# Block-sparse attention with a soft mixture of experts: value products with two heads in one matmul

## The chip, the core and the metric

The kernel runs on one NeuronCore of a Trainium2 chip. The metric is device time in microseconds (us) of one execution. The core has five engines with queues of their own: PE (TensorE, matmuls; its weight loads are listed apart as PEld), DVE (VectorE), ACT (ScalarE), POOL (GpSimd) and SP, which here only issues DMAs. They wait for one another on semaphores. PE multiplies a stationary operand (`lhsT`, loaded as weights) with a moving operand (`rhs`) whose columns stream through; contraction runs over the partitions of both, and results go to PSUM, eight banks of 512 float32 numbers for each of the 128 partitions. A product with fewer than 128 rows or weight columns uses a part of the array, a tile, and products in different tiles can run at the same time.

## The reference

Inputs are float32: `q`, `k`, `v` of shape (4, 8, 768, 64) (batches, heads, positions, head dimension) and, for the experts, `phi` (512 x 32), `w1` (8 x 512 x 1024), `w2` (8 x 1024 x 512).

```python
scores = scale * np.matmul(q, k.transpose(0, 1, 3, 2))
mask = (abs(blk_i - blk_j) <= 1) | (blk_i in (0, 23)) | (blk_j in (0, 23))
mask |= kb in sampled_blocks[qb]              # three random blocks for each query block
attn = softmax(where(mask, scores, -1e9)) @ v # heads side by side: x, 3072 x 512
logits = x @ phi
d = softmax(logits, axis=0)                   # over all 3072 rows
slot_input = d.T @ x                          # 32 slots of 512, four for each expert
slot_out[e] = relu(slot_input[e] @ w1[e]) @ w2[e]
out = softmax(logits, axis=1) @ slot_out
```

The softmaxes carry an epsilon of 1e-9. Positions are cut into 24 blocks of 32. Query blocks 0 and 23 see every key (dense); the other 22 see blocks 0 and 23, their neighbours and three sampled ones, at most eight blocks.

## The kernel before, in words

**Units.** The eight heads are four pairs; partitions 32p to 32p+31 belong to p = 0 to 3, and r = 0, 1 names the head of a pair, so one pass over r handles four heads. For every batch b there are 4 dense units (r and j, j being query block 0 or 23) and 22 sparse ones (g = 0 to 10, a pair of neighbouring query blocks, and r). `units` (L233 to L250) puts them in order: eight mixed ones by `ORDER0` or `ORDER`, then sparse ones alone. Outer blocks t = 0 to 5 are 128 rows of x: t = 0 holds the dense query blocks and the pair g = 0, each other t holds two pairs g, that is four query blocks.

**Steps of a unit.** `stage_k` (L189) copies the keys of a query block to one of four buffers `kst`: own and neighbouring blocks and the edges by POOL (L196, L201), sampled ones by ACT at addresses from registers (L205). `stage_v` (L210, L216) copies the values of the three sampled blocks by POOL to one of `NVR` = 8 buffers `vrs`. `do_qk` (L270) multiplies queries and keys, 64 rows (the head dimension of one head) to a matmul, for both r at once (L288; L277 for dense). `do_soft` takes the maximum on DVE (L304) and the exponential on ACT (L307). `do_tr` transposes 32 x 32 blocks on DVE (L326; L323 for dense), so that keys lie on partitions.

**Value products.** `av_half` (L353 to L382) computes, for one b, t and r, the product of the transposed weights with the values: for edge blocks and the pair's own two blocks (L362) 64 query rows at once, for the remaining neighbour and the sampled ones (L380) 32. The value table has 65 columns, the last one being 1, so that the sum of weights comes with it. `av_dense` (L344, L349) does it over all 24 blocks. Every matmul contracts the 32 keys of one block for one head: 32 rows, 65 columns. `avt` is one set of four banks, bank p for head p, used by all of them in turn. `av_out` (L335 to L342) adds epsilon, takes reciprocals and writes x for this r, on DVE.

**Experts' front.** `moe_front` (L385 on) takes each finished block of x: four transposes (e1, L394, evacuated by DVE), logits (e2, L439, copied by ACT to `lp`), two sums (e3, L446 and L447), the exponential on ACT and a running maximum (e3b), a transpose (e4, L463), and the product with x (e5, L478, added on DVE at L481). Some of its results lie in unused columns of `avt`.

**Order.** PE's and DVE's order is written out by hand in the loop at L568: in step n there are the value products of the unit before (`X[0]`), parts of the experts' front (`EOFF`, `X[1]`, `X[2]`), QK two units ahead, transposes of unit n, softmax. POOL, ACT and SP are ordered by the scheduler. `KSTEP` = 5 and `VSTEP` = 2 say how many units ahead keys and values are staged; at g = `KEARLY` = 4 keys and values of the next batch are loaded (`load_k`, `load_v`), in the last batch weights in their place.

**Memory and weights.** `pk` holds two tiles `ktile` and two `vtile`. The experts' weights are 64 tiles of 128 x 1024 numbers (512 KB). `NPRE` = 22 have a place of their own and are loaded during attention; three each go early to the tile `ktile` and the tile `vtile` that fall free in the last batch; the rest follows when attention ends, into `NLB` = 9 tiles `lwb` in the attention's memory and into tiles that fall free. Then come the two layers of the experts (L730, L738) and the combination (L830).

Of the kernel before, what the change touches and what calls it, by code (L numbers as in the profile page):

```python
# [21 lines left out]
P = 128  # L22
# [7 lines left out]
NBZ = NB + 1  # L30
EPS = 1e-9
# [3 lines left out]
NKST, NVR, NQ, NPTD = 4, 8, 3, 1  # L35
PB, PTB, XB = 4, 5, 2
# [4 lines left out]
KSTEP, VSTEP, EARLY = 5, 2, 4  # L41
# [13 lines left out]
NPRE, NLB = 22, 9  # L55
KW = 3
# [9 lines left out]
def attn_moe_kernel(ctx, tc, qT, kT, vtab, sampled, phi, w1, w2, out):  # L66
# [8 lines left out]

    wsrc = [w1[e, hf] for hf in range(2) for e in range(NE)]
# [12 lines left out]
    def load_wk(m, tag):  # L89
        t = pk.tile([P, KW, WP], F32, name="kw", tag=tag)  # L90
        for j in range(KW):
            load_w(m + j, None, t[:, j, :])
# [64 lines left out]
    vrs = [pst.tile([P, NR, 2 * D1], F32, name=f"vrs{n}") for n in range(NVR)]  # L157
# [52 lines left out]
    def stage_v(b, i):  # L210
# [3 lines left out]
        vf = vtile[b].rearrange("p k r d -> p k (r d)")  # L214
        for j in range(NR):
            POOL.tensor_copy(out=st[:, j:j + 1, :], in_=vf[:, ds(vals[j], 1), :])  # L216
        return st.rearrange("p j (r d) -> p j r d", r=2)
# [36 lines left out]
    def do_stage(u):  # L254
# [4 lines left out]
        if u.r == 0 and u.g == KEARLY:  # L259
# [3 lines left out]
            else:  # L263
                for j, tag in enumerate(("ktile", "vtile")):
                    load_wk(NPRE + j * KW, tag)
# [51 lines left out]
    def do_tr(u):  # L317
# [17 lines left out]
    def av_out(b, t, r, lo, hi):  # L335
        a = avt[lo:hi]
        rs = pw.tile([P, NP], F32, tag="rs", name="rs")
        DVE.tensor_scalar(out=rs[lo:hi], in0=a[:, :, D], scalar1=EPS, scalar2=None, op0=ALU.add)  # L338
        DVE.reciprocal(out=rs[lo:hi], in_=rs[lo:hi])
        x = new_x(b, t).rearrange("p (f h d) -> p f h d", f=2, h=NP)  # L340
        DVE.tensor_tensor(out=x[lo:hi, r], in0=a[:, :, 0:D],  # L341
                          in1=rs[lo:hi].unsqueeze(2).to_broadcast([hi - lo, NP, D]), op=ALU.mult)  # L342
# [10 lines left out]
    def av_half(b, t, us, r):  # L353

        vt = vtile[b]
        for n, c in enumerate((4, 5, 1, 2)):
            for p in range(NP):
                s_ = slice(32 * p, 32 * p + 32)
                for u in us:
                    o = 32 * quad(2 * u.g + 1)  # L360
                    k = (0, NB - 1, 2 * u.g + 1, 2 * u.g + 2)[n]
                    PE.matmul(avt[o:o + 64, p, 0:D1], lhsT=u.pt[s_, c].rearrange("p j q -> p (j q)"), rhs=vt[s_, k, r, :],  # L362
                              start=(n == 0), stop=False)
        for n in range(NR + 1):
            for p in range(NP):
                s_ = slice(32 * p, 32 * p + 32)
# [552 lines left out]
```

## Time and profile before

| | |
|---|---|
| three runs | 538.02, 539.32, 540.36 us (median 539.32) |
| the profiled execution | 535.25 us, span 533.5 us |
| mean granted clock of PE | 0.734 |
| instructions | 28450 |
| DMA | 60.99 MB, 114 GB/s on average |

The page of the profile gives the busy time of each engine, the span in slices, DMA queues, the chain of work that ended last, and groups of instructions by line of the kernel. "issue" is idle time in which an engine waited for nothing that the profile shows. A float32 matmul is two records of PE and two weight loads. Counts in a row that ends with a clock, a DMA share and GB/s are those of instructions that fall in that stretch. The ends of matmuls are modelled, since they are pipelined.

### The profile page before, as it was taken

Reading aid. Unit: us, or ns where it says so; the run is one execution under the profiler, and the core shown is the slowest. Engines: PE = TensorE matmul, PEld = TensorE weight load, DVE = VectorE, ACT = ScalarE, POOL = GpSimd, SP = SyncE. Lnnn points to the kernel's source line nnn. Section 1 sums busy time; section 2 is a strip of 40 time slices with the busy share of each in tenths; the row PEclk is TensorE's granted clock in tenths of the full one; section 3 lists DMA queues with packets and bytes.
Section 4 is the critical chain, followed back from the end, with each engine's and each line's share of the span. In section 5 each row is a group of like instructions: output and inputs, shape, how many; then the busy total and the mean of one; then the engine's idle time right before and its main releaser. Section 6 shows DMA issues by size and latency. Waiting matters only on the chain.

```text
span 533.5 us, 28450 instructions
## 1 busy us (share of the span) xinstructions
PE 416.5 (78%) x12629; PEld 266.3 (50%) x12629; DVE 250.2 (47%) x677; ACT 187.0 (35%) x629; POOL 125.9 (24%) x391
## 2 busy tenths in 40 slices
PE   5697378876878877779967777979687796789980
PEld 1455255554456545545655554546555454553640
DVE  2464055533654544456464445554544673550141
ACT  2435044333234333433244444332344532120140
POOL 3511033431211323232112313331113330211000
PEclk9957576769577667775687777685877656589996
DMA  8758830132200000404000004040000021099998
GB/s 300 278 161 309 326 104 24 28 127 68 75 22 23 15 17 21 142 15 137 14 23 23 15 23 143 14 130 4 24 14 23 25 78 46 10 354 409 407 346 255
DMA packets 26510, 60.99 MB, mean 114 GB/s; under 512 B 2705, under 2 KB 15122, under 8 KB 26386
## 3 DMA queue, kind: packets, MB, share of 16 engines
q1 hardware_dynamic: 26386, 59.16, 31.8%
q8 instruction: 99, 1.62, 1.2%
q14 instruction: 25, 0.20, 0.1%
HBM read 52.86 MB, written 6.29 MB: 111 GB/s over the span
## 4 chain that ended last, share of the span: by engine, by line
PE 61%; DVE 13%; issue 13%; DMA 5%; ACT 4%; ACTq 1%; SPq 0%; DVEq 0%
PE avt L380 15%; PE s L288 11%; PE avt L362 10%; PE avt L349 7%; PE sd L277 7%; DMA w<-in_w_dram 4%; DVE nm L304 3%; PE pf L730 3%; DVE ptt L326 2%; PE mlt L446 2%; DVE ptd L323 2%; PE avt L439 2%; ACT p L307 2%; PE mxt L394 2%; DVE x L341 1%
## 5 line engine op out<-in xcount | busy, mean ns | idle before, releaser
L216 POOL COPY vrs<-vtile 128x130 f32 x264 | 68.1, 295 | 209.2 <-PE avt L380 178.8
L205 ACT ACTIVATE kst<-ktile 128x128 f32 x264 | 63.8, 300 | 142.9 <-PE s L288 125.1
L380 PE MATMUL avt<-vrs,ptt 32*32 32x65 f32 x4224 | 75.8, 271 | 43.7 <-issue 43.6
L380 PEld LDWEIGHTS avt<-vrs,ptt 32*32 32x32 f32 x4224 | 63.5, 122 | 48.5 <-issue 46.6
L288 PE MATMUL s<-kst,qc 64*32 64x256 f32 x1408 | 81.0, 511 | 7.4 <-ACT p L307 4.0
L307 ACT ACTIVATE p<-s,nm 128x256 f32<-128x256 f32 x176 | 72.0, 466 | 25.1 <-DVE rs L338 15.8
L362 PE MATMUL avt<-vtile,ptt 32*64 32x65 f32 x2816 | 59.9, 278 | 13.2 <-issue 6.1
L201 POOL TENSOR_SCALAR kst<-ktile 128x384 f32<-128x384 f32 x88 | 44.0, 512 | 96.9 <-PE s L288 96.8
L304 DVE TENSOR_REDUCE nm<-s 128x2 f32<-128x512 f32 x88 | 58.8, 669 | 17.0 <-PE s L288 16.5
L362 PEld LDWEIGHTS avt<-vtile,ptt 32*64 32x64 f32 x2816 | 49.1, 171 | 34.4 <-issue 10.7
L326 DVE STREAM_TRANSPOSE ptt<-p 128x512 f32<-128x512 f32 x88 | 61.7, 701 | 0.1
L338 DVE TENSOR_SCALAR rs<-avt 128x4 f32<-128x4 f32 (+1 forms) x56 | 8.4, 150 | 90.5 <-ACT lp L312 59.0
L314 DVE COPY d<-md 128x32 f32<-128x32 f32 x23 | 4.4, 191 | 97.2 <-PE md L463 97.2
L288 PEld LDWEIGHTS s<-kst,qc 64*32 64x32 f32 x1408 | 30.0, 132 | 36.7 <-issue 17.9
L349 PE MATMUL avt<-vtile,ptd 32*64 32x65 f32 x1536 | 37.9, 279 | 11.8 <-DVE sacc L481 6.6
L277 PE MATMUL sd<-ktile,qd 64*32 64x384 f32 x256 | 41.7, 734 | 5.9 <-DMA ktile<-in_kT_dram 5.2
L349 PEld LDWEIGHTS avt<-vtile,ptd 32*64 32x64 f32 x1536 | 36.4, 192 | 14.9 <-DVE sacc L481 7.4
L301 ACT ACTIVATE pd<-sd,nb 128x384 f32<-128x384 f32 x32 | 16.8, 576 | 52.8 <-DVE nb L298 50.6
L295 DVE TENSOR_REDUCE nm<-sd 128x1 f32<-128x384 f32 x32 | 17.1, 548 | 16.8 <-PE sd L277 16.7
L341 DVE TENSOR_TENSOR x<-avt,rs 128x256 f32<-128x256 f32 (+1 forms) x56 | 23.7, 424 | 1.9
L394 PE MATMUL mxt<-ident,x 128*128 128x128 f32 x92 | 23.2, 401 | 0.0
L380 PE MATMUL avt<-vtile,ptt 32*32 32x65 f32 x1280 | 22.4, 269 | 0.4 <-issue 0.4
(104 smaller groups left out, 369.4 us busy)
## 6 DMA issues: line engine op xcount, KB each, us to landing
w<-in_w_dram SPq DMA_DIRECT2D x52, 512.0 KB, 10.2
ktile<-in_kT_dram SPq DMA_DIRECT2D x16, 384.0 KB, 5.7
kw<-in_w_dram SPq DMA_DIRECT2D x12, 512.0 KB, 5.1
qc<-in_qT_dram SPq DMA_DIRECT2D x44, 128.0 KB, 2.1
out_dram<-ob SPq DMA_DIRECT2D x20, 256.0 KB, 4.4
vtile<-in_vtab_dram SPq DMA_DIRECT2D x4, 845.0 KB, 5.6
vtile<-in_vtab_dram SPq DMA_DIRECT2D x4, 780.0 KB, 7.5
qd<-in_qT_dram SPq DMA_DIRECT2D x4, 128.0 KB, 2.2
```

What stands on the lines that cost most here:

```text
L201: POOL.tensor_scalar(out=st[:, :, w:w + 96], in0=kv[:, :, (i - 1) * BLK:(i + 2) * BLK], scalar1=SCALE, scalar2=1.0, op0=ALU.mult, op1=ALU. ...
L205: ACT.activation(out=st[:, :, o:o + BLK], in_=kv[:, :, ds(vals[j] * BLK, BLK)], func=AF.Copy, scale=SCALE)
L216: POOL.tensor_copy(out=st[:, j:j + 1, :], in_=vf[:, ds(vals[j], 1), :])
L277: PE.matmul(u.s[n][32 * p:32 * p + 32, :], lhsT=qd[s_, p, u.j, :], rhs=kt[s_, p, 384 * n:384 * (n + 1)], start=True, stop=True)
L288: PE.matmul(u.pair_of[r].s[32 * p:32 * p + 32, j, :], lhsT=q[s_, p, j, :], rhs=kst_[s_, p, :], start=True, stop=True)
L304: DVE.tensor_reduce(out=nm, in_=u.s, axis=AX.X, op=ALU.max, negate=True)
L307: ACT.activation(out=u.p[:, hf, :], in_=u.s[:, hf, :], func=AF.Exp, bias=nm[:, hf:hf + 1], scale=1.0)
L326: DVE.transpose(out=u.pt.rearrange("p k j q -> p j k q"), in_=u.p.rearrange("p j (k q) -> p j k q", k=8))
L349: PE.matmul(avt[64:128, p, 0:D1], lhsT=u.pt[s_, k].rearrange("p j q -> p (j q)"), rhs=vt[s_, k, u.r, :], start=(k == 0), stop=(k == NB - 1))
L362: PE.matmul(avt[o:o + 64, p, 0:D1], lhsT=u.pt[s_, c].rearrange("p j q -> p (j q)"), rhs=vt[s_, k, r, :], start=(n == 0), stop=False)
L380: PE.matmul(avt[o:o + 32, p, 0:D1], lhsT=u.pt[s_, c, j, :], rhs=v_, start=False, stop=(n == NR))
L394: PE.transpose(ps[:, c, :], x[:, c * P:(c + 1) * P], ident)
```

## The change

Values lie in two buffers `vbuf`, one for even and one for odd batches, with two halves a = 0, 1 of 25 x 2 x 65 numbers on every partition. The values of p stand in half p % 2; the other half is zero. POOL writes the zeros once in each buffer, four memsets of 3250 elements on 32 partitions, and `load_v` is four DMAs instead of two, of the same bytes. A value product takes partitions 64g to 64g+63 (g = 0, 1 now counts pairs of p), so two heads, and 130 columns, the two halves side by side: each head's keys meet its own values in one half and zeros in the other. The results of the two heads lie side by side.

The transposed weights of the two pairs g of an outer block share one tile of 8 x 4 x 32 (three such tiles in place of five half as large), so that the products with the edge blocks take 128 query rows at once. `avt` becomes two sets of two banks; an outer block has one set for both r, the next block the other, and `av_out` runs once for both r (in the very last block once for each). Buffers `vrs` hold both halves; there are six instead of eight, and `VSTEP` is 1. Heads are put in another order by the layout on the host, so that x comes out as before.

Of the weights 13 tiles instead of 22 have a place of their own; early groups are three in `ktile` and six in the first `vbuf`, late ones three and six in the second, and `lwb` has 11 tiles instead of 9. `c_turn` shares tiles of the new size.

```diff
-NKST, NVR, NQ, NPTD = 4, 8, 3, 1
-PB, PTB, XB = 4, 5, 2
+NKST, NVR, NQ, NPTD = 4, 6, 3, 1
+PB, PTB, XB = 4, 3, 2
-KSTEP, VSTEP, EARLY = 5, 2, 4
+KSTEP, VSTEP, EARLY = 5, 1, 4
-NPRE, NLB = 22, 9
-KW = 3
+NPRE, NLB = 13, 11
+KW = {"ktile": 3, "v0": 6, "v1": 6}
...
+    VH = NBZ * 2 * D1
+    vbuf = [pk.tile([P, 2 * VH], F32, name=f"v{n}", tag=f"v{n}", bufs=1) for n in range(2)]
...
-    vrs = [pst.tile([P, NR, 2 * D1], F32, name=f"vrs{n}") for n in range(NVR)]
+    vrs = [pst.tile([P, 2, NR, 2 * D1], F32, name=f"vrs{n}") for n in range(NVR)]
...
-    avt = psA.tile([P, NP, 512], F32, name="avt", tag="av", bufs=1)
+    avt = psA.tile([P, 2, 2, 512], F32, name="avt", tag="av", bufs=1)
...
     def load_v(b):
-        vtile[b] = pk.tile([P, NBZ, 2, D1], F32, name="vtile", tag="vtile")
-        for k0, k1 in ((0, 13), (13, NBZ)):
-            SP.dma_start(out=vtile[b][:, k0:k1], in_=vtab[b, :, k0:k1])
+        vb = vbuf[b % 2].rearrange("p (a f) -> p a f", a=2)
+        if b < 2:
+            for p in range(NP):
+                POOL.memset(vb[32 * p:32 * p + 32, 1 - p % 2, :], 0.0)
+        for p in range(NP):
+            SP.dma_start(out=vb[32 * p:32 * p + 32, p % 2, :], in_=vtab[b, 32 * p:32 * p + 32, :])
+        vtile[b] = vb.rearrange("p a (k r d) -> p a k r d", k=NBZ, r=2)
...
-            POOL.tensor_copy(out=st[:, j:j + 1, :], in_=vf[:, ds(vals[j], 1), :])
+            POOL.tensor_copy(out=st[:, :, j:j + 1, :], in_=vf[:, :, ds(vals[j], 1), :])
...
-            u.pt = pw.tile([P, 8, 2, BLK], F32, tag="ptt", name="ptt", bufs=PTB)
-            DVE.transpose(out=u.pt.rearrange("p k j q -> p j k q"), in_=u.p.rearrange("p j (k q) -> p j k q", k=8))
+            t, n = (u.g + 1) // 2, 2 * (u.g > 0 and u.g % 2 == 0)
+            if n == 0:
+                pts[u.b, t, u.r] = pw.tile([P, 8, 4, BLK], F32, tag="ptt", name="ptt", bufs=PTB)
+            u.pt = pts[u.b, t, u.r]
+            DVE.transpose(out=u.pt[:, :, n:n + 2, :].rearrange("p k j q -> p j k q"), in_=u.p.rearrange("p j (k q) -> p j k q", k=8))
...
+    def av_mm(av, o, m, g, r, lhsT, rhs, start, stop):
+        PE.matmul(av[o:o + m, g, r * 2 * D1:(r + 1) * 2 * D1].rearrange("p (a d) -> p a d", a=2),
+                  lhsT=lhsT, rhs=rhs, start=start, stop=stop)
 
     def av_dense(u):
         vt = vtile[u.b]
+        av = new_set((u.b, "d"), u.r)
         for k in range(NB):
-            for p in range(NP):
-                s_ = slice(32 * p, 32 * p + 32)
-                PE.matmul(avt[64:128, p, 0:D1], lhsT=u.pt[s_, k].rearrange("p j q -> p (j q)"), rhs=vt[s_, k, u.r, :],
-                          start=(k == 0), stop=(k == NB - 1))
-        return lambda: av_out(u.b, 0, u.r, 64, 128)
+            for g in range(2):
+                s_ = slice(64 * g, 64 * g + 64)
+                av_mm(av, 64, 64, g, u.r, u.pt[s_, k].rearrange("p j q -> p (j q)"), vt[s_, :, k, u.r, :],
+                      k == 0, k == NB - 1)
+        return (lambda: av_out(u.b, 0, av, 64, 128)) if u.r else None
...
+        for n, c in enumerate((4, 5)):
+            for g, s_ in gs:
+                av_mm(av, 0, m, g, r, pt[s_, c, 0:m // BLK].rearrange("p j q -> p (j q)"),
+                      vt[s_, :, (0, NB - 1)[n], r, :], n == 0, False)
+        for c in (1, 2):
+            for w, u in enumerate(us):
+                for g, s_ in gs:
+                    av_mm(av, 64 * w, 64, g, r, pt[s_, c, 2 * w:2 * w + 2].rearrange("p j q -> p (j q)"),
+                          vt[s_, :, 2 * u.g + c, r, :], False, False)
         for n in range(NR + 1):
-            for p in range(NP):
-                s_ = slice(32 * p, 32 * p + 32)
-                for u in us:
-                    for j in range(2):
+            for w, u in enumerate(us):
+                for j in range(2):
+                    for g, s_ in gs:
...
-                        PE.matmul(avt[o:o + 32, p, 0:D1], lhsT=u.pt[s_, c, j, :], rhs=v_,
-                                  start=False, stop=(n == NR))
-        return lambda: av_out(b, t, r, 0, 64 * len(us))
+                        av_mm(av, 64 * w + 32 * j, 32, g, r, pt[s_, c, 2 * w + j], v_, False, n == NR)
+        return (lambda: av_out(b, t, av, 0, m)) if r else None
```

More of the change, by code (lines that the diff above doesn't have):

```diff
@@ L89, in load_wk @@
     def load_wk(m, tag):
-        t = pk.tile([P, KW, WP], F32, name="kw", tag=tag)
-        for j in range(KW):
+        k = KW[tag]
+        if tag == "ktile":
+            t = pk.tile([P, k, WP], F32, name="kw", tag=tag)
+        else:
+            t = vbuf[int(tag[1])][:, 0:k * WP].rearrange("p (k f) -> p k f", k=k)
+        for j in range(k):
             load_w(m + j, None, t[:, j, :])
@@ L263, in do_stage @@
             else:
-                for j, tag in enumerate(("ktile", "vtile")):
-                    load_wk(NPRE + j * KW, tag)
+                m = NPRE
+                for tag in EARLYW:
+                    load_wk(m, tag)
+                    m += KW[tag]
         if u.r == 1 and u.g + 1 < NG2:
@@ L333, in new_x @@
         return xt[b, t]
[L335 to L338, printed above, removed]
-        DVE.reciprocal(out=rs[lo:hi], in_=rs[lo:hi])
-        x = new_x(b, t).rearrange("p (f h d) -> p f h d", f=2, h=NP)
-        DVE.tensor_tensor(out=x[lo:hi, r], in0=a[:, :, 0:D],
-                          in1=rs[lo:hi].unsqueeze(2).to_broadcast([hi - lo, NP, D]), op=ALU.mult)
+    sets, avset = [0], {}
@@ new lines, in new_set, with av_out @@
+    def new_set(key, r):
+        if r == 0:
+            avset[key] = sets[0] % 2
+            sets[0] += 1
+        return avt[:, avset[key]]
+    def av_out(b, t, av, lo, hi, rs_=slice(0, 2)):
+        n = rs_.stop - rs_.start
+        a = av[lo:hi, :, 0:4 * D1].rearrange("p g (r a d) -> p g r a d", r=2, a=2)[:, :, rs_]
+        x = new_x(b, t).rearrange("p (g r a d) -> p g r a d", g=2, r=2, a=2)[lo:hi, :, rs_]
+        if n == 2:
+            a, x = (v.rearrange("p g r a d -> p g (r a) d") for v in (a, x))
+        else:
+            a, x = (v.rearrange("p g r a d -> p (g r) a d") for v in (a, x))
+        rs = pw.tile([P, 2, 2 * n], F32, tag="rs", name="rs")
+        DVE.tensor_scalar(out=rs[lo:hi], in0=a[:, :, :, D], scalar1=EPS, scalar2=None, op0=ALU.add)
+        DVE.reciprocal(out=rs[lo:hi], in_=rs[lo:hi])
+        DVE.tensor_tensor(out=x, in0=a[:, :, :, 0:D],
+                          in1=rs[lo:hi].unsqueeze(3).to_broadcast([hi - lo, 2, 2 * n, D]), op=ALU.mult)
@@ L351, in av_dense @@
-        return lambda: av_out(u.b, 0, u.r, 64, 128)
-    def av_half(b, t, us, r):
-        vt = vtile[b]
-        for n, c in enumerate((4, 5, 1, 2)):
-            for p in range(NP):
-                s_ = slice(32 * p, 32 * p + 32)
-                for u in us:
[L360 to L363, printed above, removed]
-        for n in range(NR + 1):
-            for p in range(NP):
-                s_ = slice(32 * p, 32 * p + 32)
-                for u in us:
-                    for j in range(2):
-                        i = 2 * u.g + 1 + j
-                        o = 32 * quad(i)
+            for g in range(2):
+                s_ = slice(64 * g, 64 * g + 64)
+                av_mm(av, 64, 64, g, u.r, u.pt[s_, k].rearrange("p j q -> p (j q)"), vt[s_, :, k, u.r, :],
+                      k == 0, k == NB - 1)
@@ L694, in load_group @@
     def load_group(tag, load=True):
-        if len(wpool) + KW <= NW:
+        if len(wpool) + KW[tag] <= NW:
             if load:
                 load_wk(len(wpool), tag)
-            wpool.extend([Group(tag)] * KW)
-    for tag in ("ktile", "vtile"):
+            g = Group(tag)
+            wpool.extend([g] * KW[tag])
+    for tag in EARLYW:
         load_group(tag, False)
@@ L713, in next_w @@
                 freed.append(pool)
-    load_group("ktile")
+    load_group(LATEW[0])
     next_w([lwb] * NLB)
-    load_group("vtile")
+    load_group(LATEW[1])
     def done_w(n):
@@ L875, in layout @@
 def layout(inputs):
-    q, k, v = inputs["q"], inputs["k"], inputs["v"]
+    heads = [4 * (p // 2) + 2 * r + p % 2 for r in range(2) for p in range(NP)]
+    q, k, v = (inputs[n][:, heads] for n in "qkv")
     a = {}
```

56 lines of the change are left out of this document (37 added, 19 removed).

## The prediction

> **What bounds the kernel now.** I read the page first, for the engines' shares.
>
> ```profile
> span 533.5 us, 28450 instructions
> ...
> PE 416.5 (78%) x12629; PEld 266.3 (50%) x12629; DVE 250.2 (47%) x677; ACT 187.0 (35%) x629; POOL 125.9 (24%) x391
> ...
> q8 instruction: 99, 1.62, 1.2%
> ```
>
> PE is the busiest by far. It executes 12629 matmul records and as many weight loads, two of each for a float32 product, and 1.62 MB of instructions come in 99 packets, 16.4 KB each: 25258 PE instructions over 99 is 255, so a packet is about 256 of them. Next a table of busy time by stage (columns: stretch and its length; busy time and count of PE, weight loads, DVE, ACT, POOL; granted clock; DMA share; GB/s). The stages are cut where a value product of a whole outer block begins.
>
> ```profile
> core 0: us, PE busy (x) PEld busy (x) DVE busy (x) ACT busy (x) POOL busy (x), PEclk, DMA share, GB/s
> 0.00:49.30 49.30, 36.33 (x756) 19.67 (x756) 22.86 (x65) 18.22 (x57) 15.60 (x52) 0.86 0.76 268
> 49.30:121.40 72.10, 52.17 (x1881) 35.06 (x1876) 31.18 (x79) 26.70 (x97) 21.19 (x68) 0.65 0.37 124
> 121.40:170.10 48.70, 38.72 (x1158) 25.49 (x1154) 24.09 (x67) 14.79 (x48) 7.75 (x25) 0.72 0.15 48
> 170.10:234.10 64.00, 51.78 (x1883) 33.37 (x1876) 31.95 (x81) 27.53 (x101) 21.49 (x68) 0.71 0.14 45
> 234.10:279.00 44.90, 38.20 (x1159) 25.49 (x1155) 24.63 (x67) 15.13 (x49) 7.76 (x25) 0.70 0.16 52
> 279.00:343.30 64.30, 51.28 (x1883) 33.08 (x1876) 31.70 (x81) 27.40 (x100) 21.38 (x68) 0.73 0.14 45
> 343.30:388.20 44.90, 36.38 (x1159) 24.50 (x1155) 24.52 (x67) 15.12 (x49) 7.73 (x25) 0.77 0.16 47
> 388.20:458.20 70.00, 54.56 (x1884) 36.10 (x1877) 38.60 (x110) 26.32 (x93) 16.38 (x52) 0.66 0.11 36
> 458.20:476.80 18.60, 15.14 (x448) 11.88 (x447) 8.14 (x34) 4.43 (x15) 3.89 (x9) 0.63 0.55 188
> 476.80:513.80 37.00, 35.77 (x426) 17.34 (x426) 7.21 (x22) 6.74 (x14) 2.77 (x5) 1.00 1.03 405
> ```
>
> Four sparse stages (72.1, 64.0, 64.3 and 70.0, together 270.4 us) hold four periods each, a period being one outer block from one value product to the next: 16.9 us on average. Between them lie three dense stages (138.5 us). In all of these PE is 72 to 85% busy, no other engine over 55%, and the clock is about 0.7. The expert stage from 476.8 is another matter: DMA is full at 405 GB/s.
>
> The waits and then the eight value products of one sparse stage show what PE's idle time is.
>
> ```profile
> PE avt L380 <- issue: 44.0, 27, 4.3
> ...
> PE mlt L446 <- ACT lp L312: 7.3, 17, 0.5
> ```
>
> ```profile
> 303.15:312.31 9.16, 8.14 (x255) 4.80 (x254) 6.71 (x15) 5.37 (x19) 4.43 (x14) 0.73 0.12 33
> 312.31:319.53 7.22, 5.34 (x256) 4.25 (x256) 1.12 (x5) 1.47 (x7) 0.59 (x2) 0.68 0.02 5
> ```
>
> ```profile
> 278.99:283.48 4.49, 2.53 (x203) 2.16 (x200) 1.94 (x4) 2.85 (x10) 0.83 (x2) 1.00 0.13 35
> 285.22:288.84 3.62, 3.45 (x194) 2.86 (x193) 0.45 (x2) 0.71 (x4) 0.35 (x2) 0.50 0.02 5
> ...
> sum 34.13, PE 24.21 PEld 20.48 DVE 10.17 ACT 13.82 POOL 6.70; mean PE 3.03 PEld 2.56 DVE 1.27 ACT 1.73 POOL 0.84
> ```
>
> 44 us of idle lie inside the value products, at L380, and nothing that the profile shows ends them. The two windows of the second fence run from one such stop's end to the next one's: 512 instructions each (255 + 254 by its edges, 256 + 256), exactly two packets. So PE has run out of instructions and waits for the next packet. A half block (192 records, 384 instructions) takes 34.13/8 = 4.27 us, of which 3.03 busy. The Trainium skill ("Runtime: NRT & Kernel Launch", Instruction fetch mechanics) agrees that fetching goes in blocks of 256 but says that the issue hides it; here the rows say that it does not.
>
> **The change, part by part.** Each product takes two heads: 64 rows, 130 columns, half of them zeros, so calls halve; the edge blocks' products take four query blocks, so there they halve again. A half block falls from 96 calls to 44 (4 + 8 + 8 + 24), 88 records, 176 instructions; a dense product from 96 to 48 calls. All of PE falls from 12629 to about 7400 records: 58 packets for 99.
>
> *The stops.* A period now issues about 960 instructions in 16.1 us and will issue some 540, two packets in a period instead of four. I take the 44 us as gone; what is late next is the array itself.
>
> *Streaming.* What does a 64-row product cost? The nearest rows are the QK products, also 64 rows by 32 columns of weights, in eight tiles of the array at once, at half and at full clock:
>
> ```profile
> 304.51 1.96 PE L288 MATMUL s<-kst,qc 64*32 64x256 f32 x32
> ```
>
> ```profile
> 265.20 1.09 PE L288 MATMUL s<-kst,qc 64*32 64x256 f32 x32
> ```
>
> Per tile that is 32 x 256 / 8 = 1024 columns: 1.06 ns a column at full, 1.91 at half clock. The dense products of before, four row groups at once:
>
> ```profile
> 260.70:265.10 4.40, 4.40 (x194) 4.32 (x193) 0.55 (x3) 1.66 (x6) 0.00 (x0) 0.66 0.13 34
> 265.10:270.10 5.00, 1.62 (x42) 0.71 (x41) 4.64 (x13) 2.46 (x9) 0.99 (x2) 1.00 0.10 26
> 270.10:274.70 4.60, 4.59 (x200) 4.53 (x206) 0.57 (x1) 0.63 (x2) 0.00 (x0) 0.63 0.02 4
> ```
>
> 192 x 65 / 4 = 3120 columns in 4.40 us at 0.66 are 0.93 ns a column at full clock. So dense products already go at the array's pace, and for them the zeros cost: 96 x 130 / 2 = 6240 columns, 5.8 us at full and 11.6 at half clock. Sparse half blocks now stream only 64 x 65 / 8 + 128 x 65 / 16 = 1040 columns, 1 to 2 us, and yet are busy for 3.03: they go at the pace of issue. After the change they have 8 x 130 / 2 + 16 x 130 / 4 + 64 x 130 / 8 = 2080 columns: 1.9 to 2.2 us at full, 3.9 at half clock. The clock thus becomes the question.
>
> The Trainium skill ("TensorEngine Tiling (Array Packing)", When to Use Tiling) speaks against this change: a contraction of 32 rows should take four row groups, one of 64 only two. By that alone every value product would double. The dense rows agree with it; the sparse rows, 3.03 us for 1 to 2 us of columns, do not.
>
> *The clock.* Windows of 3.41 us in one stretch:
>
> ```profile
> 174.96:178.37 3.41, 3.31 (x185) 2.92 (x186) 0.26 (x2) 0.71 (x4) 0.29 (x1) 0.50 0.02 5
> ...
> 181.78:185.19 3.41, 3.41 (x51) 1.71 (x44) 3.13 (x7) 2.76 (x10) 2.21 (x8) 0.50 0.12 41
> 185.19:188.60 3.41, 2.68 (x194) 2.00 (x178) 2.38 (x4) 2.73 (x10) 1.01 (x2) 1.00 0.13 43
> ```
>
> The first, a half block's 185 short records, kept the half clock though PE looks busy: by the count above they stream some 1,000 columns, 1.9 us of the 3.41 at half clock. The second, 51 long records (QK, transposes) that fill most of the array, was followed by full clock. After the change a half block fills every tile while it streams, as QK does. A period's array work is 2 x 2080 columns on the whole array, 2 x 1024 for QK and some 1,400 for the rest (by the code's shapes), about 7,600 columns, 7 us of a 12 us period at full clock. I therefore take the sparse stages at full clock nearly throughout.
>
> *A sparse period.* In the stage of 64.3 us, what is not value product is (64.3 - 34.13)/4 = 7.5 us. If all of it followed the clock it would fall to 7.5 x 0.73 = 5.5; but it holds waits (the 0.44 us for lp, among others) that grow as PE gets quicker, and DVE alone is busy 31.70/4 = 7.9 us in a period. I leave it at 7.5 and add two half blocks of 2.1 and 0.3 for new waits: 12.0 us, bounds 9.7 (5.5 + 4.2) and 13.5. Sixteen periods: 270.4 - 192 = 78 us saved (bounds 54 and 115).
>
> *Elsewhere.* Dense products: the two rows above have a clock of 0.66 and 0.63, that is, about 3 us at half before it rises. So 3 us do 1,600 columns and 4,640 take 4.3 us: 7.3 for 4.5, eight times: +22 (bounds +10, all at full, and +57, all at half). Eight half blocks outside the sparse stages, 4.27 to 2.1: -17. The first outer block's products (one pair alone, eight times) have 1950 columns, 2.5 us at 0.73, for about 2.1: +3. The output's division for r = 0, under 1 us, leaves the chain between the two dense products: -2. Elsewhere on DVE divisions fall from 56 calls to 29 wider ones and transposes keep their number; DVE is off the path, so 0. The rest of the dense stages at a somewhat better clock: -3 (0 to -15).
>
> *POOL and DMA.*
>
> ```profile
> L216 POOL COPY vrs<-vtile 128x130 f32 x264 | 68.1, 295 | 209.2 <-PE avt L380 178.8
> ...
> L196 POOL TENSOR_SCALAR kst<-ktile 128x256 f32<-128x256 f32 x16 | 6.5, 403 | 11.1 <-DMA ktile<-in_kT_dram 7.1 <-PE s L288 3.9
> ...
> L769 POOL MEMSET hT<- 128x1024 f32 x2 | 1.8, 950 | 0.0
> ```
>
> The value copies double to 260 elements: 295 to about 410 ns, 1.4 us more in a period in which POOL is busy 5.3: hidden, while the period stays over 7 us. With six buffers two units' copies must follow the block's last product; PE then has two QK products and more ahead of the next. The zeroing is 4 memsets of 3250 elements, 3.0 us each by the memset row, 12 us in a block, twice. On POOL's queue the key copies of following units stand behind it, and QK waits for them. At the start it overlaps the wait for keys (7.1 us, row above): +1. In the first batch it meets a lead of about two loop steps: +5 (0 to 12). The value load is the same bytes in four transfers and is issued well over 30 us ahead, hidden except in the first batch: 0, at most 7.
>
> Weights: 22 tiles are on the chip before the last product (13 + 3 + 6) instead of 28 (22 + 6). The expert stage is bound by DMA, so 6 tiles of 524 KB at 405 GB/s come on top: +8.
>
> **Sum:** -78 + 22 - 17 + 3 - 2 - 3 + 1 + 5 + 8 = -61. The profiled execution took 535.25 us (span 533.5), so 474; the median shown, 539.32, is 4 above it: **478**.
>
> **The rivals.** *One: the clock goes on alternating* at 0.73. With the same terms written as functions of the clock c (40 half blocks at 2.0, 16 periods' rest at 5.5, 8 dense products at 5.8, 8 first blocks at 1.85, the dense stages' rest at 53 in sum, all divided by c), the new time of these parts is 282/c against 431 now, and 12 come on top. At 0.73: -33, so 502, 506 as a median. For it: waits between PE's steps thin the windows. Against it: the array work above.
>
> *Two, slower: the zeros win.* The same sum is zero at c = 0.67. If 64-row streams do not raise the clock, and it falls to 0.62 in these stages, it gives +36: 575. Dense products at half clock alone cost 57 of that. For it: the 185-record row stayed at 0.50 with PE 97% busy, and the dense rows are already at 0.63. Against it: QK, which has the very form of the new products, is what raises the clock now. The tiling rule of the Trainium skill cited above would make this one come true.
>
> *Three: the stops are not instruction fetch* and stay: 44 back, 522. Against it: the windows of 512. The sentence of the Trainium skill cited above, that fetching is hidden, would speak for it.
>
> *Four: waits shrink with the rest* and periods go to their lower bound, 9.7: another 37 saved, 441.
>
> **How the numbers follow.** Forecast 0.60, rival one 0.18, two 0.11, three 0.05, four 0.06. The range 445 to 535 holds the forecast with its period between 10 and 13.5 and its dense products between their bounds, and rivals one and three; two and four are left out, about 0.2. The runs before spread from 538.0 to 540.4, so 0.5% is about what can be told from no change: faster 0.87, within it 0.02, slower 0.11.
>
> **What would show it.** Right: about 7,400 PE records and 58 packets; almost no issue idle at the value products; a half block of some 2 us; clock near 1 in the sparse stages and periods of 12 us; dense products of 6 to 8 us; expert stage 8 us longer. Wrong: a clock at or under 0.73 there; issue idle that stays; PE waiting on POOL's value copies in every period.

## The result and the profile after

The changed kernel takes 453.38 us (median of four runs, 452.92 to 455.31) against 538.67 beside it: a ratio of 0.849 (95% interval 0.8385 to 0.8596). Ratios, here and below, leave out runs over 1.5% above the fastest of their kernel (two of the four of the kernel before), while medians and ranges are of all runs. The profiled execution took 453.23 us, span 451.5, mean granted clock 0.961 (before: 535.25, 533.5 and 0.734).

The page of the changed kernel, its span, engines, instruction queue, POOL's copies and zeroing, and the largest group of value products:

```profile
span 451.5 us, 17924 instructions
...
PE 355.6 (79%) x7381; PEld 231.5 (51%) x7381; DVE 241.8 (54%) x596; ACT 187.4 (42%) x629; POOL 176.2 (39%) x399
...
q8 instruction: 58, 0.95, 0.9%
...
L229 POOL COPY vrs<-v 128x260 f32 x264 | 97.0, 407 | 131.9 <-PE avt L378 109.0
L378 PE MATMUL avt<-v,ptt 64*64 64x130 f32 (+2 forms) x1728 | 86.8, 300 | 16.5 <-DVE ptt L344 12.2
...
L183 POOL MEMSET v<- 32x3250 f32 x8 | 22.4, 2801 | 0.3
```

7381 records and 58 packets of instructions, as forecast; 407 ns a value copy and 2.80 us a memset (forecast 410 ns and 3.0 us). The waits of the changed kernel (engine and line, what it waited for, us in total, times, longest):

```profile
PE avt L523 <- DVE x L374: 22.9, 20, 1.9
...
PEld avt L378 <- issue: 13.2, 56, 0.6
PE avt L378 <- DVE ptt L344: 12.2, 16, 2.3
```

The row of 44.0 us of issue idle at the value products is gone; what is left for issue there is never longer than 0.6 us. PE now waits on DVE. The table by stage has the same columns as before and is cut at the same events. (The trace has records of the clock from 27.4 us on and counts 1.00 ahead of them, though 30 QK records took 1.96 us at 19.75 us, the prediction's figure for half clock; so the 1.00 of the first row is too high.)

```profile
0.00:50.36 50.36, 36.06 (x477) 21.63 (x477) 26.75 (x60) 17.62 (x56) 39.05 (x55) 1.00 0.59 153
50.36:97.40 47.04, 38.62 (x1044) 25.01 (x1044) 29.25 (x68) 26.96 (x99) 24.79 (x65) 1.00 0.60 204
97.40:138.40 41.00, 34.58 (x675) 25.26 (x675) 22.75 (x58) 15.27 (x50) 11.18 (x28) 0.96 0.24 56
138.40:186.00 47.60, 38.56 (x1046) 24.95 (x1046) 29.60 (x69) 27.42 (x100) 25.03 (x66) 1.00 0.19 59
186.00:227.00 41.00, 34.64 (x674) 25.28 (x674) 22.74 (x58) 15.12 (x49) 11.07 (x28) 0.96 0.24 56
227.00:274.50 47.50, 38.54 (x1046) 24.91 (x1046) 29.61 (x69) 27.35 (x100) 25.03 (x66) 1.00 0.19 60
274.50:315.70 41.20, 34.80 (x676) 25.38 (x676) 22.84 (x58) 15.30 (x50) 11.18 (x28) 0.96 0.28 87
315.70:372.90 57.20, 43.52 (x1042) 28.96 (x1042) 37.60 (x97) 26.60 (x93) 21.79 (x57) 0.87 0.18 60
```

The prediction's terms can be put together by stage and set beside this (what follows 372.9 is 78.6 us, against 75.3 before):

| stages | before | after | change | forecast |
|---|---|---|---|---|
| start | 49.3 | 50.4 | +1.1 | +7.4 (two dense products, two first blocks, memset) |
| four sparse | 270.4 | 199.3 | -71.1 | -73 (-78, and +5 for the memset) |
| three dense | 138.5 | 123.2 | -15.3 | +1.3 (+16.8 - 12.8 + 2.3 - 2 - 3) |
| the rest | 75.3 | 78.6 | +3.3 | +3.8 (+8 - 4.2) |
| sum | 533.5 | 451.5 | -82.0 | -61 |

So the sparse stages came out near the forecast in sum, and three quarters of what the forecast missed lies in the dense stages. Two half blocks and a dense product of the changed kernel, each cut from its first product to the end of its last:

```profile
239.16:241.59 2.43, 2.43 (x92) 1.93 (x96) 1.71 (x3) 2.01 (x9) 1.25 (x3) 1.00 0.16 54
242.95:245.46 2.51, 2.51 (x90) 2.01 (x89) 0.45 (x2) 0.72 (x4) 0.40 (x1) 1.00 0.02 7
```

```profile
207.53:213.09 5.56, 5.56 (x98) 5.38 (x97) 1.16 (x6) 1.66 (x6) 0.00 (x0) 1.00 0.09 27
```

A half block is 2.47 us with no idle time inside (2.1 forecast; 4.27 before), a dense product 5.56 (7.3 forecast), and the granted clock stands at 1.00 from their first to their last product. In the first three batches a period is 11.8 us (12.0 forecast).

### The profile page after: what moved, and what is told of

Its sections match the earlier page's. It is cut to its first block, busy times and chain, and to the rows that moved or that the text cites. A ratio compares the mean times of both kernels' runs of the same rounds, so it can differ in the third digit from the quotient of the medians.

```text
span 451.5 us, 17924 instructions
## 1 busy us (share of the span) xinstructions
PE 355.6 (79%) x7381; PEld 231.5 (51%) x7381; DVE 241.8 (54%) x596; ACT 187.4 (42%) x629; POOL 176.2 (39%) x399
## 4 chain that ended last, share of the span: by engine, by line
PE 42%; DVE 27%; DMA 12%; ACT 9%; issue 5%; ACTq 2%; SPq 0%
PE avt L378 30%; DMA w<-in_w_dram 7%; DVE nm L319 6%; DVE ptt L344 6%; ACT p L322 5%; DVE x L374 4%; PE sd L292 4%; PE mlt L491 2%; DVE ptd L338 2%; ACT kst L218 2%; DMA kw<-in_w_dram 2%; DMA ktile<-in_kT_dram 2%; PE s L303 2%; ACTq L197 1%; DMA out_dram<-ob 1%
## 5 line engine op out<-in xcount | busy, mean ns | idle before, releaser
L229 POOL COPY vrs<-v 128x260 f32 x264 | 97.0, 407 | 131.9 <-PE avt L378 109.0
L378 PE MATMUL avt<-v,ptt 64*64 64x130 f32 (+2 forms) x1728 | 86.8, 300 | 16.5 <-DVE ptt L344 12.2
L322 ACT ACTIVATE p<-s,nm 128x256 f32<-128x256 f32 x176 | 71.9, 468 | 24.1 <-DVE nm L319 11.7
L378 PEld LDWEIGHTS avt<-v,ptt 64*64 64x64 f32 (+2 forms) x1728 | 57.9, 139 | 46.3 <-DVE ptt L344 22.8
L303 PE MATMUL s<-kst,qc 64*32 64x256 f32 x1408 | 60.8, 393 | 5.6 <-ACT p L322 4.5
L378 PE MATMUL avt<-v,ptd 64*64 64x130 f32 x768 | 46.2, 276 | 10.6 <-DVE sacc L526 7.0
L378 PE MATMUL avt<-vrs,ptt 64*32 64x130 f32 x2112 | 51.5, 285 | 0.0
L378 PEld LDWEIGHTS avt<-v,ptd 64*64 64x64 f32 x768 | 44.2, 136 | 12.9 <-DVE sacc L526 7.8
L378 PEld LDWEIGHTS avt<-vrs,ptt 64*32 64x32 f32 x2112 | 41.5, 110 | 0.4
L292 PE MATMUL sd<-ktile,qd 64*32 64x384 f32 x256 | 31.1, 533 | 8.6 <-DMA ktile<-in_kT_dram 6.5
L316 ACT ACTIVATE pd<-sd,nb 128x384 f32<-128x384 f32 x32 | 16.8, 577 | 47.2 <-DVE nb L313 47.2
L523 PE MATMUL avt<-x,d 128*32 128x128 f32 x192 | 10.2, 284 | 23.5 <-DVE x L374 22.9
L183 POOL MEMSET v<- 32x3250 f32 x8 | 22.4, 2801 | 0.3
L523 PEld LDWEIGHTS avt<-x,d 128*32 128x32 f32 x192 | 3.8, 107 | 34.7 <-DVE x L374 31.8
## 6 DMA issues: line engine op xcount, KB each, us to landing
w<-in_w_dram SPq DMA_DIRECT2D x37, 512.0 KB, 10.2
```

Of the source, the lines that this page charges most:

```text
L183: POOL.memset(vb[32 * p:32 * p + 32, 1 - p % 2, :], 0.0)
L229: POOL.tensor_copy(out=st[:, :, j:j + 1, :], in_=vf[:, :, ds(vals[j], 1), :])
L292: PE.matmul(u.s[n][32 * p:32 * p + 32, :], lhsT=qd[s_, p, u.j, :], rhs=kt[s_, p, 384 * n:384 * (n + 1)], start=True, stop=True)
L303: PE.matmul(u.pair_of[r].s[32 * p:32 * p + 32, j, :], lhsT=q[s_, p, j, :], rhs=kst_[s_, p, :], start=True, stop=True)
L316: ACT.activation(out=u.p[n], in_=u.s[n], func=AF.Exp, bias=nb, scale=SCALE)
L322: ACT.activation(out=u.p[:, hf, :], in_=u.s[:, hf, :], func=AF.Exp, bias=nm[:, hf:hf + 1], scale=1.0)
```

## The experiments

The theory after the result: the gain comes of fewer PE instructions (no stops for fetching, less issue), and the zeros, dear as streaming, pay for themselves by holding the clock. What sets the new period was open. Twelve kernels were run; each time stands beside runs of the kernel before on the same chip (534.9 to 539.3 us median).

### Instructions put back, twice

First with one-column products, 52 to a half block, in front of the sparse value products (cut from the edit: the loop, without the places that call it):

```diff
+        for _ in range(pads):
+            PE.matmul(av[o:o + BLK, g, r * 2 * D1:r * 2 * D1 + 1], lhsT=lhsT[:, 0:BLK], rhs=zero,
+                      start=False, stop=False)
```

> The changed kernel with 52 products of one zero column added to every half block (384 PE instructions again, as before the change; they add zeros from the empty 25th block, 32 rows of weights, almost nothing to stream). Theory that the stops were instruction fetch: a period issues some 950 instructions again, nearly four packets at 3.5 to 4 us each, so periods of 13.4 to 15 us for 11.8 and idle named issue inside the value products; 485 to 515 us. Rival, that the stops had to do with the old tiles, banks or row groups: the small products cost only their issue, 0.2 us in a half block, about 461 us, and no stops.

Measured: 896.17 us, ratio 1.684 (1.666 to 1.7025). Neither theory. The timeline of this kernel (start, duration, operation, shape) shows why:

```profile
300.05 0.26 PE L379 MATMUL avt<-v,ptt 64*32 64x1 f32 x2
300.24 0.69 PE L381 MATMUL avt<-v,ptt 64*64 64x130 f32 x2
300.86 0.26 PE L379 MATMUL avt<-v,ptt 64*32 64x1 f32 x2
```

One product of 64 x 64 tiles and one pad of 64 x 32 come every 0.81 us, here at half clock, and none overlaps the next. In the changed kernel products of one shape overlap: a dense product's 48 of 64 x 64 tiles take 5.56 us at full clock, 0.12 us each. So what costs is the change of tile shape back and forth. The Trainium skill ("TensorEngine Tiling (Array Packing)", Key Properties) says that switching the tiling mode drains the engine; the rows agree and give a size. The run thus said nothing of instruction fetch. The second kernel has 48 pads to a half block, only where the shape is 64 x 32 already (the loop is that of the first, and the last line of the call gives the number of pads):

```diff
-                        av_mm(av, 64 * w + 32 * j, 32, g, r, pt[s_, c, 2 * w + j], v_, False, n == NR)
+                        av_mm(av, 64 * w + 32 * j, 32, g, r, pt[s_, c, 2 * w + j], v_, False, n == NR,
+                              (1, 2, 2, 1)[n], vt[s_, 0, NB, r, 0:1])
```

> The changed kernel with 48 extra one-column zero products in each half block of a sparse tile, all of the 64-row, 32-column shape and placed within the stretch of products that already has that shape (they add zero, so nothing else changes): 184 records and 368 instructions of the queue per half block instead of 88 and 176, and hardly any streaming (1 column each). Theory (instructions that have to be fetched set the pace once a stretch asks for more than about 256 in 3.5 to 4 us, the spacing of the instruction packets where the kernel before stood still): a half block then needs about 5.2 us instead of 2.45, with stops of 0.5 to 2 us at instruction counts that are multiples of 256 within it, some 94 instruction packets, and 44 half blocks x 2.5 make 540 to 575 us. Rival (a record only costs its issue, 10 to 12 ns, and the stops of the kernel before came from its 32-row tiles): 96 records x 11 ns = 1.1 us per half block, no stops at multiples of 256, 495 to 510 us. A third reading (the first pads were dear only through the change of tile shape, and pads within one shape are nearly free): 453 to 470.

Measured: 558.96 us, ratio 1.0388 (1.0277 to 1.0499): slower than the kernel before, with zeros, banks and order of the changed kernel and a clock of 0.907. Its page (engines, instruction packets), then windows: the stretch from the end of one stop to the start of the next, that stop itself, and a half block without one:

```profile
PE 449.2 (80%) x11541; PEld 313.7 (56%) x11541; DVE 241.3 (43%) x596; ACT 187.5 (34%) x629; POOL 176.4 (32%) x399
...
q8 instruction: 90, 1.47, 1.1%
```

```profile
339.33:342.84 3.51, 0.00 (x0) 0.00 (x0) 0.00 (x0) 0.00 (x0) 0.00 (x0) 0.79 0.61 209
329.63:339.33 9.70, 8.06 (x255) 5.17 (x254) 6.91 (x15) 5.85 (x20) 6.22 (x16) 1.00 0.40 117
288.03:292.03 4.00, 4.00 (x188) 3.48 (x192) 1.83 (x3) 2.76 (x10) 0.63 (x2) 1.00 0.17 39
```

Between two stops lie 509 instructions (255 and 254, counted by the edges), two packets again, and in the stop of 3.5 us no engine runs anything. Counted over the whole trace, 18 idle times of PE (over 80 ns) fall on one and the same position modulo 256 in PE's list of instructions (in order of time, those of its sequencer included), 20.7 us together. The same count gives 41 and 57.7 us for the kernel before, at the very same position; in the changed kernel that position has 1.0 us and no other over 5.6. So the stops are the fetch of instructions, and fewer instructions take them away. (That the issue hides the fetch, as the Trainium skill has it in "Runtime: NRT & Kernel Launch", Instruction fetch mechanics, doesn't hold in these rows either.) But most of the cost is plainer: a half block without a stop takes 4.00 us instead of 2.47, which is 16 ns for each of the 96 records added, not 11. The 4160 records of pads at 16 ns are 67 us, the stops 21, and 18 of the 106 us remain, with the clock lower. The theory's total holds, but in good part by another cost than the one it named; its 5.2 us for every half block doesn't. What is shown is that with nearly the old number of instructions (23082 for 25258) the whole gain is gone, though zeros, banks and order stay.

### The zeros, taken away and put into the kernel before

The changed kernel with half the columns (`rhs[:, 0]` alone, 65 columns: it leaves out one head of every two, whose part of `avt` is set to zero once), and the kernel before with 130 columns in its 32-row products (both heads of a pair, of which it uses one):

> The changed kernel with the first 65 of the 130 columns of each value product only (the second head of each pair of p is left out, its part of x stays zero): same calls and instructions, half the streaming. If the zero columns are mere cost and the clock does not need them: clock stays near 1.0, dense products 2.9 instead of 5.6 us, half blocks about 1.5 instead of 2.5, periods 10.8 to 11.3 as DVE's chain holds them, 410 to 425 us. If the zero columns are what keeps the clock up: clock back to about 0.75, periods of 12 or more, 445 to 460 us.

> The kernel before with 130 columns in every value product (the values of both r, of which one is used): the old number of instructions and four row groups, but the array work of the changed kernel. If array work sets the clock and the stops are instruction fetch: clock over 0.9, half blocks of 2.4 us busy with stops that stay, periods of 13.5 to 15 us, dense products 5.6; 480 to 500 us, quicker than before although it streams twice as much. If array work does not set the clock: dense products about 8 us and half blocks longer, 555 to 575 us.

Measured: 434.85 us, ratio 0.8181 (0.8082 to 0.828), clock 0.873; and 541.64 us, ratio 1.0137 (1.0035 to 1.0239), clock 0.863. Of the first, a half block, a period and two dense products:

```profile
238.50:240.35 1.85, 1.85 (x92) 1.62 (x96) 1.71 (x3) 1.41 (x7) 0.82 (x2) 1.00 0.25 71
238.50:249.48 10.98, 8.48 (x265) 5.64 (x265) 7.35 (x18) 6.68 (x26) 6.18 (x17) 1.00 0.10 28
281.98:285.00 3.02, 3.02 (x98) 2.95 (x97) 0.81 (x5) 1.66 (x6) 0.00 (x0) 1.00 0.00 0
115.22:120.45 5.23, 5.23 (x98) 5.16 (x97) 0.54 (x3) 1.66 (x6) 0.00 (x0) 0.54 0.08 25
```

Half the columns take 0.6 us off a half block and 2.5 off a dense product, at the same clock. With the clock held that would be 16 x 0.8 (periods) + 8 x 2.54 = 33 us; 18.5 came. The rest went to the clock: the same dense product takes 3.02 at full and 5.23 at 0.54. The result lies between the two expectations, since the zeros both cost and hold the clock. In sum they cost more than they bring: they don't pay for themselves, as the theory had it, but are the price of two heads in one product. The run also bears on what a half block is made of. 88 records with 1040 columns still take 1.85 us, 21 ns a record, and 1040 columns less saved 0.6 us, so some two thirds of the 1.85 are not streaming.

In the kernel before with twice the columns the clock rises from 0.734 to 0.863, and nothing is gained. PE is busy for 437.9 us (416.5 before), with the same 12629 records. Its wait for issue at the value products (before: 44.0 us):

```profile
PE avt L380 <- issue: 29.1, 19, 3.7
```

By the count of positions its stops are 31 and 38.2 us (41 and 57.7 before). The added columns cost time of their own: the dense products of its third dense stage take 5.57 and 7.23 us for 4.48 and 4.60, the eight half blocks of its third sparse stage 38.3 for 34.1. So the run doesn't show what the clock alone is worth; what it shows is that a fuller array without fewer instructions raised the clock and not the speed. Fewer instructions without a fuller array (the 65 columns) are fast even at a clock of 0.873.

### One set of banks

```diff
-            avset[key] = sets[0] % 2
+            avset[key] = 0
```

> The changed kernel with one set of two banks instead of two. If the second set hides nothing that is on the path (the experts' product already waits for the division in the changed kernel's trace): 453 to 457 us. If it carries part of the gain: over 460 us, with new waits of value products for the division.

Measured: 453.19 us (452.33 to 453.8), ratio 0.8489 (0.841 to 0.8569). The second set is worth nothing here: before the next block's products PE waits on DVE in any case.

### What the new period waits for

Three kernels: the sets as two tiles (`avt` a list of two), the transposition of the sparse weights placed ahead of the evaluation in DVE's order, and both.

```diff
+        if n >= 0 and not units[n].dense:
+            do_tr(units[n])
         later = run(X[0], n) + run(X[1], n)
...
-            do_tr(u)
+            if u.dense:
+                do_tr(u)
```

> The changed kernel with its two sets of banks as two tiles of their own instead of one tile of two sets, so that waits between the sets can be told apart by the program. Theory (the 1.02 us for which the output products stand before DVE's x of the other set comes of the one shared tile): that wait goes, 20 x up to 1.0 us; the next late thing is the score products' and the transposition's chain on DVE, so that 0.3 to 0.6 of each 11.78 us stays: 441 to 449 us. Rival (the products really need x's engine order, since DVE's later work is what ends last): 452 to 455, no change.

> The changed kernel with the sparse units' transposition on DVE put ahead of the evaluation of the tile (it then runs while PE makes the second half block's products, when DVE idles 2.1 to 2.2 us). Theory (the period of 11.78 us is set by a chain through DVE: sums, transposition, x, then the output products, the score products, and the next half block's wait): 0.70 us leaves the chain in each of some 22 periods, 437 to 443 us. Rival (PE is bound by its own products in sum): the idle time only moves, 450 to 454 us.

> Both at once: two tiles for the sets, and the transposition ahead. If the two waits lie on one chain one behind the other, the gains add up: 430 to 440 us; if they are two ways of ending the same wait, the better of the two alone, 437 to 446.

Measured: 452.63 (ratio 0.8434, 0.8354 to 0.8514), 455.16 (0.8479, 0.841 to 0.8548) and 452.6 us (0.8455, 0.8386 to 0.8523). None gained. With two tiles the products at L523 no longer wait for x, but the transposes behind them (L439) do, and the period stays at 11.8 us. With the transposition ahead most periods fall to 11.2, near the 0.7 us less that were expected, and the time doesn't. The third sparse and the third dense stage of the kernel with the transposition ahead (47.5 and 41.2 us in the table of the changed kernel):

```profile
226.71:271.80 45.09, 38.63 (x1044) 24.84 (x1044) 29.82 (x69) 26.65 (x100) 24.39 (x64) 1.00 0.19 59
271.80:317.37 45.57, 39.17 (x674) 28.46 (x674) 22.58 (x58) 15.24 (x49) 11.75 (x30) 0.85 0.26 83
```

2.4 us are gained in the one and 4.4 lost in the next, at a clock of 0.85 instead of 0.96. In the clock's records the half clock comes in stretches of 3.4 us and multiples of it: 3.4 us of it in this dense stage of the changed kernel, 10.2 and 3.4 with the transposition ahead. That raised the question whether the clock, or something that makes PE wait, rules the last batch too, whose periods are 11.8, 13.9, 15.7 and 15.9 us.

Next the clock was to be held by products that nobody reads, in the places where PE waits, in the kernel with two tiles and in the one with both edits (cut from the edit: the product, without the four places that call it):

```diff
+    def warm(out, n):
+        PE.matmul(out, lhsT=ident, rhs=ident[:, 0:n], start=True, stop=True)
```

> The changed kernel with its two sets of banks as two tiles, and with products whose result nobody reads (identity times identity, 128 rows by 128 columns of weights, 48 to 128 columns streamed) where PE waits in each sparse period: two ahead of the output's transposition (0.66 us of wait there), one ahead of the half block's first product (0.64 us) and one ahead of the product with lp (0.44 us); some 380 columns on the whole array, about 1.4 us at full clock in a period of 11.78. Theory (the granted clock goes by how much of the array streams in windows of 3.41 us, and the last batch's periods of 13.9, 15.7 and 15.9 us come of windows that fell just short): the clock stays at 1.0 from the first sparse stage to the last, the last batch's periods come to 11.8 to 12.3, and the start of the dense stages loses its 1 us: 440 to 446 us, clock 0.98 or more. Rival one (the last batch is long because of its own waits, and the clock falls there as a consequence): clock up, time 451 to 455. Rival two (the extra products stand in PE's way): 455 to 470.

> The same extra products with the transposition ahead of the evaluation as well (periods of 11.2 us instead of 11.8 at full clock, which were paid back by a clock of 0.83 in a dense stage and in the last batch). Theory (with the clock held, the shorter periods show in the time): 428 to 438 us. Rival (PE waits so little there that the extra products lengthen the periods by most of their 1.4 us): 440 to 455.

Measured: 467.26 us (459.36 to 469.84; ratio 0.8621, 0.8542 to 0.87) and 455.3 us (0.8494, 0.8456 to 0.8532), clocks 0.95 and 0.944. The theory fell. The first and the last batch of the kernel with two tiles and the extra products:

```profile
50.89:102.99 52.10, 45.54 (x1077) 30.62 (x1076) 29.24 (x68) 26.81 (x98) 25.96 (x67) 0.97 0.52 184
325.89:382.24 56.35, 47.88 (x1075) 32.78 (x1074) 37.38 (x98) 26.48 (x92) 21.50 (x56) 0.91 0.19 61
```

The clock dropped in the last batch as before, and the batch is as long as before but for 0.9 us. In the second and third batch the periods stayed at 11.7 to 11.9 (one of 12.9), so the extra products are nearly free there. The first batch got 5 us longer (47.0 in the changed kernel), with periods of 15.6 and 13.2; PE stands still in it for 2.45 us that the profile names issue, at the very position modulo 256 of the stops above. Why that stop came back is open. PE's waits in the last batch (1.1 us for p, 0.7 for `sacc` and 0.7 for the transposed weights in one period) remain in spite of the filler, and all three hang on DVE. DVE's timeline of the changed kernel in the second period of the last batch:

```profile
335.86 0.28 DVE L546 TENSOR_REDUCE cm<-lst 128x4 f32<-128x128 f32 x1
336.17 0.55 DVE L547 TENSOR_TENSOR lst<-lst,cm 128x128 f32<-128x128 f32 x1
336.64 0.68 DVE L319 TENSOR_REDUCE nm<-s 128x2 f32<-128x512 f32 x1
...
338.44 0.26 DVE L553 TENSOR_REDUCE cm<-lst 128x4 f32<-128x128 f32 x1
338.74 0.17 DVE L554 TENSOR_SCALAR cm<-cm 128x4 f32<-128x4 f32 x1
338.94 0.18 DVE L555 RECIPROCAL cm<-cm 128x4 f32<-128x4 f32 x1
339.16 0.66 DVE L556 TENSOR_TENSOR lst<-lst,cm 128x128 f32<-128x128 f32 x1
```

These are the combine weights' softmax (`c_soft`, `c_norm`), which the order by hand puts into the last batch: 2.1 us in this period, 0.8 of it ahead of a maximum and a transposition and 1.3 ahead of the next ones, all of which PE's next steps need. Moved to where DVE idles in the dense stages:

```diff
-    for j, g in enumerate((0, 1, 2, 5)):
+    Y = {}
+    for g in range(3):
+        Y[N // B * (g + 1) + 3] = lambda g=g: c_soft(g)
+        Y[N // B * (g + 1) + 5] = lambda g=g: c_norm(g)
+    for j, g in ((3, 5),):
...
         for f in run(X[2], n):
             f()
+        if n in Y:
+            Y[n]()
```

> The changed kernel with the combine weights' softmax of the first three groups of outer blocks (reductions, differences and products on DVE, 0.24 to 0.69 us each) moved out of the last batch's periods into the dense stages, where DVE stands idle for 4.5 to 5 us while the dense products run. Theory (the last batch's second to fourth periods, 13.9, 15.7 and 15.9 us against 11.8, are long because DVE has 2.1 to 2.7 us more to do ahead of the maxima and the transposition that PE waits for; the clock falls there only as a consequence): those three periods come back to 11.8 to 12.5, the clock there is at or near 1.0, the dense stages stay at 41 us: 442 to 447 us. Rival (the clock falls there by itself, as windows happen to lie): the periods stay at 13.5 or more, 450 to 454 us.

> The same move, with the two tiles and the transposition ahead of the evaluation (11.2 us a period at full clock, with a clock of 0.82 in the last batch and in one dense stage, 452.6 us). Theory (DVE's order sets PE's waits, and the clock follows the waits): the last batch's periods come to 11.2 to 11.8 and the gain of 0.6 us a period shows in the sum: 434 to 442 us. Rival (shorter periods thin out the next windows as before): the clock stays at or under 0.93, 443 to 453 us.

Measured: 448.81 us (446.06 to 449.07), ratio 0.8335 (0.8297 to 0.8374), and 441.41 us (439.7 to 444.42), ratio 0.8219 (0.8177 to 0.8261). The last batch's four periods, of the changed kernel and with the move alone:

```profile
315.66:327.48 11.82, 9.68 (x265) 6.29 (x265) 7.47 (x18) 7.11 (x28) 5.65 (x16) 1.00 0.08 25
327.48:341.35 13.87, 10.57 (x266) 6.48 (x266) 9.32 (x24) 7.85 (x30) 7.66 (x19) 0.88 0.07 22
341.35:357.01 15.66, 11.21 (x265) 7.53 (x265) 10.92 (x30) 6.76 (x23) 5.38 (x14) 0.89 0.08 20
357.01:372.87 15.86, 12.06 (x245) 8.68 (x245) 9.91 (x28) 4.92 (x15) 3.10 (x9) 0.76 0.44 158
```

```profile
318.35:330.19 11.84, 9.68 (x265) 6.29 (x265) 7.48 (x18) 7.11 (x28) 5.66 (x16) 1.00 0.09 25
330.19:341.96 11.77, 9.68 (x265) 6.29 (x265) 7.36 (x18) 6.93 (x27) 6.19 (x17) 1.00 0.10 26
341.96:353.73 11.77, 9.67 (x265) 6.28 (x266) 7.37 (x18) 6.48 (x24) 5.98 (x16) 1.00 0.05 15
353.73:367.70 13.97, 9.69 (x245) 6.77 (x245) 10.29 (x28) 4.81 (x15) 4.09 (x12) 0.90 0.56 190
```

The second and third periods are back at 11.77 us and at full clock; only the last, which still holds the fourth group's softmax, has 14.0. The batch is 7.9 us shorter. The whole is 4.9 us shorter by the spans, 446.6 against 451.5: in that execution the start, which the edit doesn't touch, was 1.9 us longer, and the three batches between 0.8. So the periods came out as the theory had them, and the time, 448.81, 2 us above its 442 to 447; whether the longer start is chance isn't shown. With the transposition ahead and two tiles the last batch takes 47.4 us for 57.2 and the gain of the shorter periods shows, though one dense stage still loses clock: 441.41 us, faster than both kernels, some 3% under the changed one (0.8219 to 0.849 of the kernel before).

## Why the prediction was right or wrong

**Right in direction; 25 us (5%) too slow.** 478 was forecast, 453.4 came, in the range. The mechanism held where the stops and the clock are concerned; the sizes of several terms didn't, and some of their errors cancel.

**The stops.** Right: 58 packets, and the issue idle gone. The padded kernel, in which they come back with the instructions, makes fetching the cause; rival three is out. By the count of positions the stops were 57.7 us of the kernel before, more than the 44.0 of one line. They are not all that instructions cost: of the 106 us that the pads added, some 67 went to the records themselves, by the estimate above.

**Streaming.** The term of 2.1 us for a half block was too small: 2.47. It came from columns alone; the kernel with half the columns still takes 1.85 us. Forty half blocks at 0.37 cost 15 us more than forecast. The rest of a period was too large by somewhat more: 11.78 - 2 x 2.47 = 6.84 us against 7.8. The period, 11.78 for 12.0, was right by two errors that cancel, which is luck.

**The clock.** Right that fuller tiles raise it (before with 130 columns: 0.734 to 0.863) and that without the zeros it sinks (0.873 for 0.961). Rivals one and two are out: the clock didn't alternate at 0.73, and the tiling rule that a contraction of 32 rows wants four row groups describes the dense products, 1.1 us dearer, but not the whole. Rival four's period of 9.7 us didn't come either: DVE's chain holds it at 11.8, and at 11.2 with the transposition ahead. What the clock is worth by itself isn't shown: in the one run that raised it with the old number of instructions the added columns took what it gave.

**Dense products.** This is the term that was mis-sized: 22 us were forecast, from "about 3 us at half before it rises". That came from the rows of before; yet the same text had the clock at 1 in the stage ahead, so there was no half clock left to rise from. Only the very first, with QK ahead of it still at half-clock pace, took 7.28; the other seven took 5.56, under the lower bound of 5.8. For the six in dense stages that is 10.4 us. The dense stages' rest, -3 (0 to -15), took the remainder, 6 us more (8, since six half blocks there cost 2 more than forecast), at a clock of 0.96 for 0.70 to 0.77.

**POOL.** The +5 for the first batch didn't come: all eight memsets ran in the start, the last of them until 38.5 us, and the first batch's periods are as long as the others', 11.7 to 11.8 us. But the +1 in the start was too small, as its own terms say: four memsets are 12 us, and the wait that was to hide them 7.1. POOL's first key copy in the kernel before, then the memsets and the first key copy in the changed one:

```profile
8.81 0.40 POOL L196 TENSOR_SCALAR kst<-ktile 128x256 f32<-128x256 f32 x1 [7.13 <-DMA ktile<-in_kT_dram]
```

```profile
4.06 8.48 POOL L183 MEMSET v<- 32x3250 f32 x3
12.63 0.41 POOL L209 TENSOR_SCALAR kst<-ktile 128x256 f32<-128x256 f32 x1
```

The key copies begin 3.8 us later, and the first dense product 4.0 (23.93 us for 19.91). From there to the first sparse stage the changed kernel took 26.4 us for 29.4, so that of +7.4 for the start +1.1 was left; why that part got quicker wasn't taken apart.

**DVE at nothing.** "DVE is off the path, so 0" was wrong for the last batch: with PE quicker, 2.1 us of softmax on DVE lengthened three periods, and the clock went with them. The move shows 7.9 us of it. The rows of before had a sign of it, for the softmax stands at the same place in its order: its last sparse stage has 6.9 us more of DVE work than the third and took 70.0 us for 64.3. In the sum over the sparse stages (-71 for -73) the 9.2 us by which the last batch missed 48 were hidden by the +5 that didn't come and by the shorter periods of the other batches, luck again.

**Weights.** +3.3 us after the sparse stages for +3.8.

## What to carry to other kernels

Where short matmuls leave PE standing at counts that are multiples of 256 instructions, fewer instructions can be worth more than the columns they waste: here 42% fewer records, at twice the columns for each value product, saved 15%. Before a new clock is put into a sum, carry it through every stage: a product that starts at full clock has no ramp to pay. And when the busiest engine gets quicker, go through the other engines' orders for work that was placed where it used to be covered.

## What was not expected of the hardware

- **Change of tile shape.** Alternating products of 64 x 64 and 64 x 32 tiles came at 0.81 us a pair at half clock; 48 products of 64 x 64 without a change came at 0.12 us each at full clock.
- **Price of a record.** Without stops a one-column product of 64 rows still took 16 ns for each of its two records, at full clock; the stream of one column was not what it cost.
- **The clock gives and takes.** 0.6 us less in every period was paid back by one to three more stretches of 3.4 us at half clock in the dense stage behind it. Products in PE's gaps didn't keep the clock up in the last batch; moving the work that PE waited for did, in two of its three long periods.
